# Layer norm beside two projection blocks: where statistics, transposes and weight splits stand in the order of work

## The chip, the cores and the metric

The kernel runs on one core of a Trainium2 chip. The metric is the device time of one execution in microseconds (us); lower is better. Three runs of the kernel before gave 1754.59, 1755.76 and 1760.3 us; the median is 1755.76 us. A fourth execution was recorded by the hardware profiler; it took 1754.43 us, and its span, from the first to the last instruction, is 1752.7 us.

## The reference

One sequence of 2048 rows of 512 values goes through attention with 32 heads of 16 and then through a two-layer network with SiLU, each behind a layer norm and each added to its input:

```python
x = A_x
h = x + _A_ref(_layernorm(x, axis=-1), A_wqkv, A_wo)
h2 = h + _B_ref(_layernorm(h, axis=-1), B_w1, B_w2)
```

`_A_ref` multiplies by `wqkv` (512 x 1536), splits into q, k and v, applies softmax over the scores, multiplies by v and by `wo`. The change concerns only the first layer norm and the product with `wqkv`.

## The kernel before

**Numbers.** Products are done on pairs of tiles in the engine's rounded 32-bit form: each operand is split into a high part, made by a copy on ScalarE (`act("copy", ...)`), and a low part, made by a subtraction on VectorE (`low`). A product takes three matmuls for each of four chunks: high by high, low by high, high by low (`product`, line 101). So one 128x512 result costs 12 matmuls.

**The stage around the change** (lines 281 to 422). The 2048 rows are treated in four blocks `b` of 512 rows, and each block in four tiles `t` of 128 rows. The rows of a block lie in `xts[b]`; only two such buffers exist, so blocks 0 and 2 share one (it is the memory of `ks[2]`), and blocks 1 and 3 the other. A tile has to pass four steps before the projections of its block can use it:

- `statistics` (line 147): two instructions on VectorE (`st`, then `mv`), then two small ones on GpSimd (`rs`, an addition and a power).
- `normalize` (line 158): one instruction on VectorE, which needs `rs`, and writes the rows in place.
- the transposes of `turn_x` (lines 161 and 363): four on TensorE into the PSUM tile `ps_tr`,
- a copy on ScalarE into `xth[b]` and a subtraction on VectorE into `xtl[b]`.

While block `b` is projected, the rows of block `b + 1` are put through these four steps. A block has six units `n`: two projections of group 0, 128 key columns and 128 query columns (`("qk", 1)` for k and `("qk", 0)` for q, 12 matmuls each with the whole 512 rows of `xth[b]` and `xtl[b]` as the streamed operand), and four for v (`("v", t)`, 12 matmuls each, with one tile's columns of `xth[b]` and `xtl[b]` as weights). Block 0 does the four v units first, the others the two qk units first. After a qk unit, ScalarE writes `sh` and VectorE writes `sl` from the PSUM tile, and both are stored to device memory; after unit `k == 0` the heads' rows are read back with `load_q` and `load_k`. From block 1 on, each v unit is followed by `burst(4)`: four score products (`ps_m`, four PSUM banks of five) and four row maxima on VectorE (`mx`, line 206). The results of the projections and of the transposes take turns in three PSUM banks.

**Weight splits.** `split_qk(n)` (line 314) splits columns of `wqkv` for group `n // 2`, query (`n` even) or key (`n` odd): one copy on ScalarE (`wqk_h`) and one subtraction on VectorE (`wqk_l`). Splits 1 and 0 are done ahead of the loop. The six others were taken from a list behind units 3, 4 and 5 of blocks 0 and 1. They are needed in the next stage (line 424), which projects groups 1 to 3. The unsplit weights lie in the tail of `va`, the tile that holds v: the query columns under the places of row chunks 8 to 12, the key columns under those of 12 to 15, so a v unit of block 2 or 3 may write only when the splits under it are done. One `memset` on GpSimd (line 422) fills a column of ones in `va` behind the loop.

**What sets the order.** Every instruction of TensorE, VectorE, ScalarE, GpSimd and the DMA queue on SyncE is kept in program order within its engine (`pin`, `dve`, `act`, `pool`, `mm`, `tr`, `dma`), so the order of the calls in the loop is the order on each engine. Engines wait for each other by semaphores.

**The next stage** (line 424) projects the remaining groups, with four score products and maxima behind every seven matmuls (`BESIDE_A = 7, 4`).

Of the kernel before, what the change touches and what calls it, by code (L numbers as in the profile page):

```python
# [28 lines left out]
NG = 2 * D // P  # L29
# [30 lines left out]
def attention_mlp_kernel(ctx: ExitStack, tc: tile.TileContext, x, wqkv, wo, w1, w2, out):  # L60
# [12 lines left out]
    def pool(op, *a, **k):  # L73
        tc.keep_in_program_order(getattr(nc.gpsimd, op)(*a, **k))  # L74
# [5 lines left out]
    def act(fn, *a, **k):  # L80
        pin(getattr(nc.scalar, fn)(*a, **k))  # L81

    def dve(fn, *a, **k):
        pin(getattr(nc.vector, fn)(*a, **k))  # L84
# [4 lines left out]
    def low(dst, src, high, engine="dve"):  # L89

        if engine == "pool":
            pool("tensor_tensor", dst, src, high.bitcast(F32), ALU.subtract)
        else:
            dve("tensor_tensor", dst, src, high.bitcast(F32), ALU.subtract)
# [52 lines left out]
    def statistics(rows):  # L147

        st = small.tile([P, 6], F32, name="st", bufs=5)
        mv = small.tile([P, 2], F32, name="mv", bufs=5)  # L150
        rs = small.tile([P, 1], F32, name="rs", bufs=5)
        dve("bn_stats", st, rows)
        dve("bn_aggr", mv, st)
        pool("tensor_scalar", rs, mv[:, 1:2], EPS, None, op0=ALU.add)
        pool("tensor_tensor", rs, rs, expo, ALU.pow)
        return mv, rs

    def normalize(dst, rows, mv, rs):
        dve("tensor_scalar", dst, rows, mv[:, 0:1], rs, op0=ALU.subtract, op1=ALU.mult)

    def turn(src, dst_h, dst_l):

        ps = bank("ps_tr").rearrange("p (c n) -> p c n", n=P)
        for c in range(4):
            tr(ps[:, c, :], src[:, c * P:(c + 1) * P], ident)
        act("copy", dst_h, ps)
        low(dst_l, ps, dst_h)
# [10 lines left out]
    def load_k(i, k, lo=0, n=S):  # L178
        a, j = HEADS[k]
        h = 4 * (i % 8) + 2 * a + j  # L180
        dma(ks[i % RING][64 * j:64 * j + 48, a, lo:lo + n], kd[:, h * DH:(h + 1) * DH, lo:lo + n])

    def load_q(i, k):
        a, j = HEADS[k]
        h = 4 * (i % 8) + 2 * a + j
        lo = i // 8 * 512
        dma(qs[i % RING][64 * j:64 * j + 48, a, :], qd[:, h * DH:(h + 1) * DH, lo:lo + 512])
# [58 lines left out]
    def tick():  # L246
        at["step"] += 1
        for fn, a in agenda.pop(at["step"], ()):
            fn(*a)
# [19 lines left out]
    def burst(n):  # L269
        for _ in range(n):  # L270
            one_max()
# [9 lines left out]
    with ExitStack() as pa:  # L281
# [18 lines left out]
        def load_x(b, parts=1):  # L300
            n = 4 // parts
            for t in range(0, 4, n):
                r0 = b * 512 + t * P
                dma(xts[b][:, t:t + n, :], x[r0:r0 + n * P, :].rearrange("(t p) d -> p t d", p=P))
# [9 lines left out]
        def split_qk(n):  # L314
            g, key = divmod(n, 2)
            raw = raw_qk[key][:, :, g * P:(g + 1) * P]
            cols = slice(key * D + g * P, key * D + (g + 1) * P)
            act("copy", wqk_h[:, :, cols], raw)
            low(wqk_l[:, :, cols], raw, wqk_h[:, :, cols])

        def measure():

            ps = bank("ps_sq")
            mm(ps[:, :NG], ones, sq, start=True, stop=True)
            dve("tensor_reduce", qk_s, ps[:, :NG], axis=AX.X, op=ALU.add)
            pool("tensor_scalar", qk_s, qk_s, 1e-30, None, op0=ALU.add)
            pool("tensor_tensor", qk_s, qk_s, expo, ALU.pow)
            dve("tensor_scalar", qk_s, qk_s, TOP / 23.0, None, op0=ALU.mult)
            dve("tensor_scalar", qk_s.bitcast(U32), qk_s.bitcast(U32), 0x7F800000, None, op0=ALU.bitwise_and)
            dve("reciprocal", qk_e, qk_s)  # L330
            dve("scalar_tensor_tensor", qk_e, qk_e, SCALE, qk_e, op0=ALU.mult, op1=ALU.mult)
            pin(nc.scalar.reg_load(qk_f, qk_e[:1, :].bitcast(U32)))

        def project_qk(b, n, beside=None):

            g, key = divmod(n, 2)
            cols = slice(key * D + g * P, key * D + (g + 1) * P)
            ps = bank("ps_qk")
            weave(product(ps, lambda c: wqk_h[:, c, cols], lambda c: wqk_l[:, c, cols],
                          lambda c: xth[b][:, c, :], lambda c: xtl[b][:, c, :], DC), beside)  # L340
            sh = xp.tile([P, 512], F16, name="sh")
            sl = xp.tile([P, 512], F16, name="sl", bufs=2)
            if beside:

                t = scaled[b]
                act("mul", t, ps, qk_s)
                act("copy", sh, t)
                pool("tensor_tensor", sl, t, sh, ALU.subtract)
            else:
                act("mul", sh, ps, qk_s)  # L350
                dve("scalar_tensor_tensor", sl, ps, qk_s, sh, op0=ALU.mult, op1=ALU.subtract)
            d = (kd if key else qd)[:, g * P:(g + 1) * P, b * 512:b * 512 + 512]
            hs, ls = (slice(0, 3, 2), 1) if key else (slice(0, 2), 2)
            dma(d[hs].rearrange("s d n -> d s n"), sh[:, None, :].to_broadcast([P, 2, 512]))
            dma(d[ls], sl)

        def project_v(b, t):
            ps = bank("ps_v")
            run(product(ps, lambda c: xth[b][:, c, t * P:(t + 1) * P], lambda c: xtl[b][:, c, t * P:(t + 1) * P],
                        lambda c: wv_h[:, c, :], lambda c: wv_l[:, c, :], DC))  # L360
            act("copy", va[:, 4 * b + t, :, 0:DH], ps.rearrange("p (h d) -> p h d", d=DH))

        def turn_x(b, t):
            turn(xts[b][:, t, :], xth[b][:, :, t * P:(t + 1) * P], xtl[b][:, :, t * P:(t + 1) * P])
# [10 lines left out]
        found = [statistics(xts[0][:, t, :]) for t in range(4)]  # L375
# [9 lines left out]
        for n in range(NG):  # L385
            square(n)

        splits = list(range(2, NG))
        for b in range(NB):
            units = [("qk", 1), ("qk", 0)]  # L390
            vs = [("v", t) for t in range(4)]
            found = {}
            for n, (kind, k) in enumerate(vs + units if b == 0 else units + vs):
                tick()
                if b == 0 and n == 3:
                    measure()
                if kind == "v":
                    project_v(b, k)
                else:
                    project_qk(b, k)  # L400
                    if k == 0:
                        for i in range(2):
                            for h in range(4):
                                if b == 0:
                                    load_q(i, h)
                                load_k(i, h, b * 512, 512)
                if b > 0 and n > 1:
                    burst(4)
                if b + 1 < NB:
                    rows = xts[b + 1]  # L410
                    if n < 4:
                        found[n] = statistics(rows[:, n, :])
                    if 0 < n < 5:
                        normalize(rows[:, n - 1, :], rows[:, n - 1, :], *found.pop(n - 1))
                    if n > 1:
                        turn_x(b + 1, n - 2)
                if n > 2 and b < 2 and splits:
                    split_qk(splits.pop(0))
                if n == 0 and b + 2 < NB:
                    load_x(b + 2)  # L420
        assert not splits
# [2 lines left out]
        for g in range(1, NG // 2):  # L424
            for m, (b, key) in enumerate([(b, 1) for b in range(NB)] + [(b, 0) for b in range(NB)]):
# [4 lines left out]
                n = 8 * g + m - 12  # L430
# [183 lines left out]
    found = {}  # L614
# [57 lines left out]
    def maxima(g):  # L672

        i, c = divmod(g, KC)
        if g < LAG:
            return 0
        ready = min(ITEMS, i + RING - (0 if c == KC - 1 else 1)) * 64
        rate = max([(64 * (n + 1) - BESIDE * sum(g <= m <= KC * n for m in marks) - at["done"])
                    / max(1, KC * n - AHEAD - g) for n in range(i + 1, ITEMS)] or [0])
        if ready < END:  # L680
            rate = min(rate, (ready - at["done"]) / (KC - 1 - c or KC))
        at["due"] += max(0, rate)
        n = max(0, min(4, int(at["due"]), ready - at["done"]))
        at["due"] -= n
        return n

    fixed_rows(RING - 1)
    for g in range(groups):
# [10 lines left out]
        if i in (8, 16, 24):  # L699
            b, n = i // 8 - 1, c - OUTPUT  # L700
# [13 lines left out]
        n = maxima(g)  # L714
# [43 lines left out]
```

## Time and profile before

| | before |
|---|---|
| median of three runs | 1755.76 us |
| profiled execution | 1754.43 us |
| its span | 1752.7 us |
| TensorE busy | 1699.7 us (97%) |
| VectorE busy | 1472.0 us (84%) |
| ScalarE busy | 1263.3 us (72%) |
| GpSimd busy | 208.4 us (12%) |
| mean granted TensorE clock | 0.992 |

In the profile PE is TensorE, PEld its weight loads, DVE VectorE, ACT ScalarE, POOL GpSimd and SP SyncE. A row of the timeline gives the start in us from the beginning of the span, the duration, the engine, the line, the operation, output and inputs, the count, and in square brackets how long the engine had been idle and what ended the wait. Matmuls are pipelined: their durations overlap, and the distance of two starts is what one costs in a stream. PEclk is the clock that TensorE was granted, as a share of full speed.

### The profile page before, as it was taken

The page shows a single profiled execution, that of the slowest core. Times are in us where ns is not written, and L with a number is a line of the kernel's source. Part 1 is how long each engine was busy: PE and PEld are TensorE (multiplying, and loading weights), DVE is VectorE, ACT ScalarE, POOL GpSimd, SP SyncE. Part 2 cuts the span into 40 slices and gives each one's busy share as a digit, 9 for nine tenths or more (in the row PEclk, how much of TensorE's full clock was granted, in tenths as well). Part 3 has the DMA queues.
Part 4 walks back from the last instruction along what each step waited for, and adds up shares of the span by engine and source line. Part 5 has one row for each costly group of instructions (what it writes and reads, how often), then busy time and mean ns, then how long its engine had stood idle before and what let it go on. Part 6 is the DMA issues. An engine that isn't in the chain of part 4 may idle for free.

```text
span 1752.7 us, 28228 instructions
## 1 busy us (share of the span) xinstructions
PE 1699.7 (97%) x10466; PEld 654.2 (37%) x10466; DVE 1472.0 (84%) x2456; ACT 1263.3 (72%) x2507; POOL 208.4 (12%) x216
## 2 busy tenths in 40 slices
PE   7899999999999999999999999999999999999899
PEld 6655422222245532222245532222245532221377
DVE  6889899999978889999978899999978889994243
ACT  4223499999963369999963269999963279999643
POOL 2112210000033300000033300000033200000000
PEclk9999999999999999999999999999999999999999
DMA  6233311111113111111213111111222111100232
GB/s 183 91 87 137 113 36 44 38 39 48 51 52 100 57 45 32 35 41 44 58 48 100 55 48 30 35 45 40 61 69 82 49 45 34 36 8 11 64 90 74
DMA packets 102210, 103.10 MB, mean 59 GB/s; under 512 B 20344, under 2 KB 78776, under 8 KB 102072
## 3 DMA queue, kind: packets, MB, share of 16 engines
q1 hardware_dynamic: 102072, 101.30, 19.8%
q8 instruction: 82, 1.34, 0.3%
q14 instruction: 56, 0.46, 0.1%
HBM read 77.86 MB, written 17.30 MB: 54 GB/s over the span
## 4 chain that ended last, share of the span: by engine, by line
PE 46%; ACT 33%; DVE 18%; DMA 1%; issue 1%; SPq 1%; POOL 0%; ACTq 0%; POOLq 0%; DVEq 0%
ACT pt L81 31%; PE pv L67 20%; DVE mx L206 13%; PE ps_s L67 9%; PE ps_m L67 6%; PE ps_acc L67 5%; PE ps_wo L67 2%; DVE gl L84 2%; PE ps_v L67 2%; PE ps_qk L67 1%; ACT pvs L81 1%; DVE ot L84 1%; SPq L87 1%; PE ps_tr L70 1%; DMA w<-in_B_w_dram 0%
## 5 line engine op out<-in xcount | busy, mean ns | idle before, releaser
L206 DVE TENSOR_REDUCE mx<-ps_m 128x1 f32<-128x512 f32 x2048 | 1280.4, 683 | 114.2 <-PE ps_m L67 87.8
L81 ACT ACTIVATE pt<-ps_s 128x512 f32<-128x512 f32 x2048 | 1017.7, 646 | 31.9 <-PE ps_m L67 31.4
L67 PE MATMUL ps_s<-qs,ks 64*128 64x512 f16 x2048 | 549.9, 380 | 10.6 <-ACT pt L81 2.4
L67 PE MATMUL ps_m<-ks,qs 48*128 48x512 f16 x2048 | 531.1, 381 | 11.6 <-DVE mx L206 8.9
L67 PE MATMUL pv<-pt,va 128*17 128x512 f32 x4096 | 539.0, 599 | 0.9
L67 PEld LDWEIGHTS <-ks 64*128 64x128 f16 x2048 | 152.4, 94 | 549.9 <-issue 443.5
L67 PEld LDWEIGHTS pv<-pt,va 128*17 128x17 f32 x4096 | 68.8, 95 | 240.3 <-issue 225.9
L67 PEld LDWEIGHTS <-qs 48*128 48x128 f16 x2048 | 122.1, 94 | 82.8 <-issue 77.1
L81 ACT ACTIVATE g<-pv 128x512 f32<-128x512 f32 x52 | 31.1, 597 | 146.3 <-PE pv L67 146.3
L74 POOL TENSOR_TENSOR ot<-ot,den 128x512 f32<-128x512 f32 x15 | 19.1, 1275 | 938.3 <-DMA den<-dr 938.3
L84 DVE TENSOR_TENSOR gl<-g,gh 128x512 fp32r<-128x512 f32 x56 | 59.0, 1053 | 44.1 <-ACT gh L81 44.1
L67 PE MATMUL ps_acc<-w2h,gh 128*128 128x512 f32 x224 | 92.3, 412 | 0.0
L67 PE MATMUL ps_acc<-w2l,gh 128*128 128x512 f32 x224 | 91.6, 409 | 0.0
L81 ACT CAST w2h<-w 128x512 fp32r<-128x512 f32 x56 | 34.8, 621 | 75.2 <-POOL w1l L74 38.7
L67 PE MATMUL ps_acc<-w2h,gl 128*128 128x512 f32 x224 | 88.1, 393 | 0.0
L67 PE MATMUL pv<-hth,w1l 128*128 128x512 f32 x208 | 86.6, 416 | 0.0
L67 PE MATMUL pv<-htl,w1h 128*128 128x512 f32 x208 | 82.8, 398 | 0.0
L67 PE MATMUL pv<-hth,w1h 128*128 128x512 f32 x208 | 82.8, 398 | 0.0
L74 POOL TENSOR_TENSOR w1l<-w,w1h 128x512 fp32r<-128x512 f32 x42 | 54.7, 1301 | 165.1 <-ACT w1h L81 154.8
L81 ACT ACTIVATE ks<-ps_qk,qk_s 128x512 f32<-128x512 f32 x24 | 16.5, 689 | 70.4 <-PE ps_qk L67 70.4
L74 POOL TENSOR_TENSOR w2l<-w,w2h 128x512 fp32r<-128x512 f32 x42 | 53.6, 1277 | 59.2 <-ACT w2h L81 59.2
L67 PE MATMUL ps_qk<-xtl,wqk_h 128*128 128x512 f32 x128 | 52.8, 413 | 3.4 <-DVE xtl L84 3.4
(99 smaller groups left out, 1162.6 us busy)
## 6 DMA issues: line engine op xcount, KB each, us to landing
w<-in_B_w_dram SPq DMA_DIRECT2D x112, 256.0 KB
ks<-kd SPq DMA_DIRECT2D x120, 192.0 KB
qs<-qd SPq DMA_DIRECT2D x128, 48.0 KB
kd<-sh SPq DMA_DIRECT2D x16, 256.0 KB
qd<-sh SPq DMA_DIRECT2D x16, 256.0 KB
ot<-pvs SPq DMA_DIRECT2D x128, 32.0 KB
den<-dr SPq DMA_DIRECT2D x128, 32.0 KB
hx<-in_A_x_dram SPq DMA_DIRECT2D x16, 256.0 KB
```

The source lines that it names most:

```text
L67: tc.keep_in_program_order(nc.tensor.matmul(*a, **k))
L70: tc.keep_in_program_order(nc.tensor.transpose(*a))
L74: tc.keep_in_program_order(getattr(nc.gpsimd, op)(*a, **k))
L81: pin(getattr(nc.scalar, fn)(*a, **k))
L84: pin(getattr(nc.vector, fn)(*a, **k))
L87: pin(nc.sync.dma_start(*a))
L206: pin(nc.vector.tensor_reduce(mx[i][:, j, a, qt, kb:kb + 1], ps, axis=AX.X, op=ALU.max))
```

## The change

```diff
-        splits = list(range(2, NG))
+        splits = {(0, 3): 2, (0, 4): 4, (0, 5): 6, (1, 5): 3, (3, 0): 5, (3, 1): 7}
+
+        first_ln = {n: (range(4)[n:n + 1], range(4)[max(0, n - 1):n], range(4)[max(0, n - 2):max(0, n - 1)])
+                    for n in range(6)}
+        other_ln = {0: ((0, 1), (0,), ()), 1: ((2, 3), (1,), (0,)), 2: ((), (2,), (1,)), 3: ((), (3,), (2,)),
+                    4: ((), (), (3,)), 5: ((), (), ())}
         for b in range(NB):
...
                 if b + 1 < NB:
                     rows = xts[b + 1]
-                    if n < 4:
-                        found[n] = statistics(rows[:, n, :])
-                    if 0 < n < 5:
-                        normalize(rows[:, n - 1, :], rows[:, n - 1, :], *found.pop(n - 1))
-                    if n > 1:
-                        turn_x(b + 1, n - 2)
-                if n > 2 and b < 2 and splits:
-                    split_qk(splits.pop(0))
+                    stats, norms, turns = (other_ln if b else first_ln)[n]
+                    for t in stats:
+                        found[t] = statistics(rows[:, t, :])
+                    for t in norms:
+                        normalize(rows[:, t, :], rows[:, t, :], *found.pop(t))
+                    for t in turns:
+                        turn_x(b + 1, t)
+                if (b, n) in splits:
+                    split_qk(splits.pop((b, n)))
                 if n == 0 and b + 2 < NB:
                     load_x(b + 2)
```

Block 0 keeps its layer-norm order (`first_ln` gives for every unit what the old conditions gave). In blocks 1 and 2 the statistics of tiles 0 and 1 stand in unit 0 with the normalisation of tile 0, those of tiles 2 and 3 in unit 1 with the normalisation of tile 1; the transposes of tiles 0 to 3 stand in units 1 to 4 instead of 2 to 5. Block 0 still makes three splits in units 3 to 5, now 2, 4, 6 (the query columns) instead of 2, 3, 4. Block 1 makes one (3, in unit 5) instead of three (5, 6, 7 in units 3 to 5). The last two, 5 and 7, stand in units 0 and 1 of block 3. On TensorE the four transposes of a tile therefore stand ahead of a v unit's 12 matmuls and its four score products, where they stood behind them. No instruction is added or removed.

## The prediction

> **What bounds the kernel now.** I read the page first, then the busy time in stretches of 20 us (the stretch, its length, then the busy time of PE, PEld, DVE, ACT and POOL with their instructions, the granted clock, the busy share of the DMA engines, GB/s).
>
> ```profile
> span 1752.7 us, 28228 instructions
> PE 1699.7 (97%) x10466; PEld 654.2 (37%) x10466; DVE 1472.0 (84%) x2456; ACT 1263.3 (72%) x2507; POOL 208.4 (12%) x216
> ```
>
> ```profile
> 40.00:60.00 20.00, 17.51 (x87) 11.78 (x85) 18.24 (x35) 6.94 (x12) 3.76 (x8) 1.00 0.45 138
> 60.00:80.00 20.00, 19.33 (x86) 14.20 (x87) 13.98 (x27) 4.90 (x8) 4.49 (x9) 0.91 0.22 71
> 80.00:100.00 20.00, 18.24 (x83) 12.84 (x82) 12.05 (x20) 3.73 (x6) 0.25 (x1) 1.00 0.16 54
> 120.00:140.00 20.00, 20.00 (x93) 11.50 (x92) 20.00 (x35) 5.72 (x9) 5.28 (x5) 1.00 0.33 109
> ```
>
> The 97% says nothing of the place that changes. That is about 35 to 105 us, blocks 1 to 3. There TensorE has holes, and from 60 to 80 its clock is at 0.91; afterwards VectorE is full. The chain of waits (start, us, what) shows which of them sets the time:
>
> ```profile
> 60.58 6.91 PE ps_qk L67 x22
> ...
> 85.64 5.30 PE ps_qk L67 x22
> ...
> 104.48 12.05 DVE mx L206 x20
> ```
>
> Through blocks 2 and 3 the chain is TensorE's projections; from 104.48 it is VectorE's row maxima without a break. What block 3 finishes sooner, that run starts sooner, and everything behind it moves with it.
>
> **What the change removes: the two block ends.** At both, TensorE waits for the copy and the subtraction of the last tile (`xth`, `xtl`). Its timeline at the ends of blocks 1 and 2, and at the end of block 3, which has no transposes:
>
> ```profile
> 55.69 0.61 PE L67 MATMUL ps_m<-ks,qs 48*128 48x512 f16 x4
> 56.39 0.66 PE L70 MATMUL ps_tr<-ident,ks 128*128 128x128 f32 x4
> 57.73 0.51 PE L67 MATMUL ps_qk<-xth,wqk_h 128*128 128x512 f32 x1 [0.68 <-ACT xth L81]
> ...
> 60.58 0.50 PE L67 MATMUL ps_qk<-xtl,wqk_h 128*128 128x512 f32 x1 [2.13 <-DVE xtl L84]
> ...
> 67.33 0.39 PE L67 MATMUL ps_v<-wv_h,xth 128*128 128x512 f32 x1
> ...
> 81.95 0.61 PE L67 MATMUL ps_m<-ks,qs 48*128 48x512 f16 x4
> ...
> 83.82 0.50 PE L67 MATMUL ps_qk<-xth,wqk_h 128*128 128x512 f32 x1 [0.68 <-ACT xth L81]
> ...
> 85.64 0.50 PE L67 MATMUL ps_qk<-xtl,wqk_h 128*128 128x512 f32 x1 [1.08 <-DVE xtl L84]
> ...
> 90.77 0.39 PE L67 MATMUL ps_v<-wv_h,xth 128*128 128x512 f32 x1
> ...
> 104.04 0.61 PE L67 MATMUL ps_m<-ks,qs 48*128 48x512 f16 x4
> ...
> 104.92 0.40 PE L67 MATMUL ps_qk<-xth,wqk_l 128*128 128x512 f32 x1
> ```
>
> Without a wait, the third matmul of a block starts 104.92 - 104.04 = 0.88 us after the last score products, plus one matmul's distance of 0.23 (the 22 matmuls from 85.64 to 90.77 take 5.13): 1.11. Block 1 took 60.58 - 55.69 = 4.89, block 2 took 85.64 - 81.95 = 3.69. Of each, 0.41 is the transposes, which only move (74.98 - 74.57 below). Lost: 4.89 - 1.11 - 0.41 = 3.37 and 3.69 - 1.11 - 0.41 = 2.17. With the transposes of tile 3 in unit 4, `xtl` of tile 3 is a whole v unit ahead of the block end, and both go.
>
> **The clock behind the first of them.** The 22 matmuls from 60.58 to 67.33 take 6.75 instead of 5.13, which is 1.62 us more, because the clock was halved (stretches of 2 us, same columns):
>
> ```profile
> 62.00:64.00 2.00, 2.00 (x6) 1.55 (x5) 0.00 (x0) 0.00 (x0) 0.00 (x0) 0.50 0.14 49
> 64.00:66.00 2.00, 2.00 (x9) 1.64 (x8) 0.60 (x1) 0.69 (x1) 0.00 (x0) 0.82 0.00 1
> ```
>
> I take these 1.62 as removed with the hole of 2.13 us ahead of them. The Trainium skill (TensorE: Matmul & The Clock Gate, HAM oscillation) gives as its abstract rule that holes under some 3.4 us don't throttle; this trace disagrees, since 2.13 us after 0.68 did. The same page (Part 1) has the activity window running freely, so that the halving would vary between runs; by that the 1.62 might be missing elsewhere, and the sum would be 1.62 smaller. Both are priced as a rival below from rows alone.
>
> **Small waits inside the units.** A unit without a wait:
>
> ```profile
> 74.03 0.61 PE L67 MATMUL ps_m<-ks,qs 48*128 48x512 f16 x4
> 74.57 0.66 PE L70 MATMUL ps_tr<-ident,ks 128*128 128x128 f32 x4
> 74.98 0.48 PE L67 MATMUL ps_v<-wv_h,xth 128*128 128x512 f32 x1
> 75.29 0.39 PE L67 MATMUL ps_v<-wv_h,xtl 128*128 128x512 f32 x1
> ...
> 78.61 0.66 PE L70 MATMUL ps_tr<-ident,ks 128*128 128x128 f32 x4
> ```
>
> Score products to transposes is 0.54; at 55.69 it is 0.70, because the normalisation is late. The transposes of tile 2 in both blocks cost about as much more. With a wait of the first score products of block 1 of like size, I take four times 0.16 = 0.63 as removed. The next unit starts 3.88 us after this one (78.61 less 0.16, less 74.57). VectorE per unit needs less than that:
>
> ```profile
> 73.79 0.52 DVE L84 TENSOR_SCALAR ks<-ks,mv,rs 128x512 f32<-128x512 f32 x1
> 74.22 0.68 DVE L84 TENSOR_TENSOR xtl<-ps_tr,xth 128x512 fp32r<-128x512 f32 x1
> 74.82 2.47 DVE L206 TENSOR_REDUCE mx<-ps_m 128x1 f32<-128x512 f32 x4
> 77.22 0.68 DVE L84 BATCH_NORM_STATS2 st<-ks 128x6 f32<-128x512 f32 x1
> ```
>
> From the normalisation to the end of the maxima it is 77.22 - 73.79 = 3.43 us, 0.45 below TensorE's 3.88, so units 2 to 5 of the changed blocks are paced by TensorE. In the old block 1 the statistics (0.84) and a split (0.60) came on top, which is why VectorE ended behind.
>
> **What the change adds: one new wait in each of blocks 1 and 2.** The transposes of tile 0 now stand in unit 1, directly behind the second qk projection, and they need tile 0's normalisation. VectorE, GpSimd and TensorE there:
>
> ```profile
> 18.78 0.69 DVE L84 BATCH_NORM_STATS2 st<-ks 128x6 f32<-128x512 f32 x1 [2.43 <-DMA ks<-in_A_x_dram]
> 20.69 0.55 DVE L84 TENSOR_SCALAR ks<-ks,mv,rs 128x512 f32<-128x512 f32 x1 [0.20 <-POOL rs L74]
> ...
> 39.79 0.68 DVE L84 BATCH_NORM_STATS2 st<-ks 128x6 f32<-128x512 f32 x1
> 40.92 0.39 PE L67 MATMUL ps_v<-wv_h,xth 128*128 128x512 f32 x1
> 41.09 0.57 POOL L74 TENSOR_TENSOR rs<-rs,expo 128x1 f32<-128x1 f32 x1
> ```
>
> Block 0 already runs the new sequence (statistics of two tiles, then a normalisation that waits for `rs`): from 18.78 to 20.69 + 0.55 = 21.24 it took 2.46 us. Started at 39.79 (it can't start sooner, `sl` of the first projection stands ahead of it), it ends at 42.25. TensorE is there at 40.92. It waits 1.33 us, and behind the transposes stand the whole first v unit and its score products, so nothing covers it. The power on GpSimd, over at 41.66, bounds it from below: 41.66 + 0.55 - 40.92 = 1.29. From above, were another 0.5 us lost on GpSimd, 1.8. Block 2 has the same order and the same 1.33. The v unit behind the transposes has a first matmul of 0.31 instead of 0.23 (75.29 - 74.98), 0.1 for each block. Added: 2 x 1.43 = 2.86.
>
> Does the new wait halve the clock? Holes of 0.68 and 1.08 us close to each other, at 83.82 and 85.64, left it at 1.00; the 2.13 at 60.58 did not. 1.33 in one piece is nearest to the first, so I take nothing; the other end is 1.62 for each block.
>
> **What the moves cost elsewhere.** On VectorE, `sl` of the second projection now follows the normalisation and starts at about 42.2, some tenths later, and its store on the DMA queue follows; in block 1 that queue still issues the reads of heads until 49 (the row of 48.35 below), so nothing waits. The first maxima come behind the statistics of four tiles, but the score products also come 1.33 + 0.41 later. On ScalarE `xth` of tile 0 goes ahead of the copy of the first v, no conflict. PSUM has three banks: the second v unit now takes the bank of the transposes just ahead, whose `xtl` I put about 0.9 us before it is needed; if late, it costs at most the lateness.
>
> In block 2 the statistics of the last block's rows are read sooner, at about 62.2 instead of 66.07. Their load is issued behind those reads:
>
> ```profile
> 48.35 0.67 SPq L87 DMA_DIRECT2D ks<-kd  x1
> ...
> 50.10 0.41 SPq L87 DMA_DIRECT2D ks<-in_A_x_dram  x1
> ```
>
> By the stretches above, DMA traffic has ebbed to 49 GB/s by 62 to 64 and is 1 GB/s from 64; the remaining trickle is the reading of heads, which is used only at the first score products. I take nothing.
>
> The splits: three in block 0 stay three, nothing. Two leave block 1, and go behind the two projections of block 3:
>
> ```profile
> 91.69 0.75 DVE L84 SCALAR_TENSOR_TENSOR sl<-ps_qk,qk_s,sh 128x512 f16<-128x512 f32 x1 [1.97 <-ACT sh L81]
> 94.01 2.49 DVE L206 TENSOR_REDUCE mx<-ps_m 128x1 f32<-128x512 f32 x4 [1.57 <-PE ps_m L67]
> ```
>
> VectorE is idle for 1.97 and 1.57 us there, and a split takes 0.60 to 0.68; ScalarE is busy 3.73 of the 20 us from 80. The copy of block 3's first v must wait for the last split, which ends at 91.69 + 0.75 + 0.68 = 93.1 on the old axis, before the first maxima. The fill of ones on GpSimd waits for the same split; GpSimd is busy 0.25 of those 20 us. Nothing for all of them; without the cover it would be 0.68 for each split.
>
> **The sum.** Removed 3.37 + 2.17 + 1.62 + 0.63 = 7.79; added 2.86; net 4.93 us. Against the profiled execution, span 1752.7 plus 1.73 around it, that is 1754.43 - 4.93 = 1749.5. The median of the runs shown is 1.33 above that execution; carried over whole, 1750.8. I forecast 1750.0, between them. The bound for a change that can be told from none, 0.3%, is 1755.76 x 0.997 = 1750.5, so the forecast lies just beyond it.
>
> **Rivals.**
>
> - *The clock takes part of it back.* The new waits halve the clock in one block (1749.5 + 1.62 = 1751.1) or both (1752.7); or the removed halving is peculiar to this execution, worth the same 1.62. For it: 1.33 lies between 1.08 and 2.13. Against: the longer sum of two holes at 82 to 86 left the clock alone, and no run shown is below the profiled one, which had the halving. About 1751.9.
> - *The start of VectorE's long run doesn't move.* If something else, such as reading the heads of block 3, sets the start at 104.48, the net gain is lost: 1754.4 to 1755.8. Against: the chain shows a v unit and its score products ahead of that run, and no DMA.
> - *Slower: the rows of the last block come late.* The place is the first statistics of block 2, now at 62.2. VectorE would stand there, with `sl` and the normalisation behind it, and TensorE before the transposes. It could be at most 66.07 - 62.2 = 3.9 us, since before the statistics ran at 66.07 without a wait. In each further hole of such length the clock is halved, 1.62 for one stretch and 3.2 for two. 3.9 + 3.2 = 7.1 against 4.93 gives 1756.6; with one halving it decides from 4.93 - 1.62 = 3.3 us of lateness on. If the new wait of block 1 also reaches its upper end (0.5 more, and 1.62), 1758.7; measured against the median that is 0.2% slower, and more if the median carries its 1.33. Against: the traffic ebbs by 64.
>
> **How the numbers follow.** The forecast has 0.72, and by its own range of 1748.0 to 1751.5 (one halving more removed in block 2, or small waits kept) 0.56 of that lies beyond 0.3% and 0.16 within. The clock rival has 0.12 and the unmoved run 0.07, both within. The slower rival, with what I don't see, has 0.09: 0.06 slower by over 0.3%, 0.03 within. Together faster 0.56, same 0.38, slower 0.06. The range, 1747.0 to 1755.0, takes in the clock's bounds and half of the unmoved run.
>
> **What would show it.** In blocks 1 and 2 one hole of about 1.3 us ahead of the transposes, released by the normalisation on VectorE, and no hole over 0.3 us at the block ends; the clock at 1.00 through 60 to 70; units of 3.9 us; the unbroken run of maxima starting near 99.6 instead of 104.48, and later landmarks as much sooner. Wrong would be: holes over 2 us at the new place, v units longer than 4 us, a wait of block 2's statistics for the DMA, or a run of maxima that starts sooner while the end doesn't move.

## The result and the profile after

The changed kernel takes 1749.97 us in the median of 13 runs (1745.81 to 1753.83); the kernel before takes 1755.76 us in the median of 13 runs (1754.59 to 1760.3). The ratio is 0.9964, 95% interval 0.9956 to 0.9972, which is 4.9 to 7.7 us. The profiled execution took 1749.97 us, 4.46 us less than the profiled one before.

The page of the changed kernel, first part:

```profile
span 1748.2 us, 28230 instructions
PE 1695.7 (97%) x10466; PEld 651.4 (37%) x10466; DVE 1471.9 (84%) x2456; ACT 1263.6 (72%) x2507; POOL 207.4 (12%) x216
```

The engines' work is the same (all five counts are equal; the two instructions more in the first line are on none of these engines). The stretches of 20 us (columns as in the prediction) show where the time left:

```profile
40.00:60.00 20.00, 18.75 (x94) 13.09 (x93) 17.62 (x34) 5.90 (x10) 3.41 (x8) 1.00 0.46 137
60.00:80.00 20.00, 18.75 (x95) 13.16 (x93) 16.84 (x32) 5.83 (x10) 3.42 (x8) 1.00 0.21 72
80.00:100.00 20.00, 20.00 (x92) 13.96 (x90) 13.24 (x22) 4.98 (x9) 1.01 (x1) 1.00 0.32 76
```

TensorE does 94 and 95 instructions in the first two stretches, where it did 87 and 86; the clock from 60 to 80 is 1.00 instead of 0.91. The chain of waits through blocks 1 and 2 (start, us, what):

```profile
35.54 5.34 PE ps_qk L67 x22
40.88 1.23 issue
42.11 0.63 PE ps_tr L70 x4
...
57.14 0.54 PE ps_m L67 x4
57.68 5.68 PE ps_qk L67 x24
...
80.16 5.67 PE ps_qk L67 x24
...
99.37 12.05 DVE mx L206 x20
```

Apart from the new waits the chain now stays on TensorE from block 1 to block 3, with no step of `xtl` at their ends. The new wait begins at 40.88. TensorE's timeline and VectorE's at that place:

```profile
40.48 0.39 PE L67 MATMUL ps_qk<-xtl,wqk_h 128*128 128x512 f32 x1
42.11 0.63 PE L70 MATMUL ps_tr<-ident,ks 128*128 128x128 f32 x4 [1.25 <-issue]
42.49 0.47 PE L67 MATMUL ps_v<-wv_h,xth 128*128 128x512 f32 x1
42.81 0.39 PE L67 MATMUL ps_v<-wv_h,xtl 128*128 128x512 f32 x1
...
57.08 0.61 PE L67 MATMUL ps_m<-ks,qs 48*128 48x512 f16 x4
57.61 0.50 PE L67 MATMUL ps_qk<-xth,wqk_h 128*128 128x512 f32 x1
57.95 0.39 PE L67 MATMUL ps_qk<-xth,wqk_l 128*128 128x512 f32 x1
58.18 0.40 PE L67 MATMUL ps_qk<-xtl,wqk_h 128*128 128x512 f32 x1
...
64.60 0.63 PE L70 MATMUL ps_tr<-ident,ks 128*128 128x128 f32 x4 [1.25 <-ACT sh L81]
```

```profile
39.56 0.68 DVE L84 BATCH_NORM_STATS2 st<-ks 128x6 f32<-128x512 f32 x1
...
41.46 0.55 DVE L84 TENSOR_SCALAR ks<-ks,mv,rs 128x512 f32<-128x512 f32 x1 [0.20 <-POOL rs L74]
```

The third matmul of block 2 follows the last score products by 58.18 - 57.08 = 1.10 us (4.89 before). The two new waits are 1.25 us each. The trace names `issue` and `sh` as what ended them, but the transposes read neither; what they need is the normalisation, which ends at 41.46 + 0.55 = 42.01, just ahead of 42.11. That this is the wait's cause is tested below, by moving the normalisation and the transposes.

The executions differ already ahead of the changed place: the granted clock first rises at 16.92 us before and at 16.18 after. So the stage is measured from the product of the sums of squares (`ps_sq`, in block 0) to the start of VectorE's long run of maxima. Before, that is 104.47 - 23.81 = 80.66 us; after, 99.36 - 23.53 = 75.83. The stage is 4.83 us shorter.

### The profile page after: what moved, and what is told of

Read it like the earlier page. It is cut to its first block, busy times and chain, and to the rows that moved or that the text cites. A ratio compares the mean times of both kernels' runs of the same rounds, so it can differ in the third digit from the quotient of the medians.

```text
span 1748.2 us, 28230 instructions
## 1 busy us (share of the span) xinstructions
PE 1695.7 (97%) x10466; PEld 651.4 (37%) x10466; DVE 1471.9 (84%) x2456; ACT 1263.6 (72%) x2507; POOL 207.4 (12%) x216
## 4 chain that ended last, share of the span: by engine, by line
PE 48%; ACT 32%; DVE 16%; issue 1%; DMA 1%; SPq 1%; ACTq 0%; POOLq 0%; POOL 0%; DVEq 0%
ACT pt L81 30%; PE pv L67 20%; DVE mx L206 12%; PE ps_s L67 9%; PE ps_m L67 6%; PE ps_acc L67 5%; PE ps_v L67 3%; PE ps_wo L67 2%; DVE gl L84 2%; PE ps_qk L67 2%; PE ps_tr L70 1%; DVE ot L84 1%; ACT pvs L81 1%; SPq L87 1%; PE ps_w L67 0%
## 5 line engine op out<-in xcount | busy, mean ns | idle before, releaser
L74 POOL TENSOR_TENSOR w2l<-w,w2h 128x512 fp32r<-128x512 f32 x42 | 53.5, 1275 | 59.5 <-ACT w2h L81 59.5
L67 PE MATMUL ps_qk<-xth,wqk_h 128*128 128x512 f32 x128 | 52.5, 411 | 0.8 <-ACT xth L81 0.8
```

Of the source, the lines that this page charges most:

```text
L67: tc.keep_in_program_order(nc.tensor.matmul(*a, **k))
```

## The experiments

"Stage" is the distance just defined, read from one profiled execution of each kernel. Each ratio is to runs of the kernel before that were made beside that kernel (medians from 1755.55 to 1756.44 us); 5 to 13 runs stand behind each median.

| kernel | stage, us | median, us | ratio to before, 95% interval |
|---|---|---|---|
| before | 80.66 | 1755.76 | |
| the change | 75.83 | 1749.97 | 0.9964 (0.9956 to 0.9972) |
| e1_order_only | 75.80 | 1750.13 | 0.9970 (0.9959 to 0.9982) |
| e2_splits_only | 77.69 | 1753.25 | 0.9984 (0.9973 to 0.9995) |
| e3_first_turn_later | 73.44 | 1749.02 | 0.9963 (0.9949 to 0.9976) |
| e4_four_statistics | 79.86 | 1753.97 | 0.9988 (0.9979 to 0.9997) |
| e5_block2_only | 79.59 | 1752.52 | 0.9984 (0.9972 to 0.9996) |
| e6_later_again | 73.41 | 1748.04 | 0.9962 (0.9949 to 0.9974) |
| e7_all_ends | 74.16 | 1749.67 | 0.9964 (0.9949 to 0.9980) |
| e8_keys_first | 72.72 | 1746.72 | 0.9946 (0.9932 to 0.9959) |

**The order of layer norm alone** (e1_order_only).

```diff
-        splits = {(0, 3): 2, (0, 4): 4, (0, 5): 6, (1, 5): 3, (3, 0): 5, (3, 1): 7}
+        splits = {(0, 3): 2, (0, 4): 3, (0, 5): 4, (1, 3): 5, (1, 4): 6, (1, 5): 7}
```

> New order of layer norm in blocks 1 and 2, but the six weight splits where they stood before (2, 3, 4 behind units 3 to 5 of block 0; 5, 6, 7 behind units 3 to 5 of block 1). My theory: with `xtl` of the last tile a unit ahead of the block end, two more splits of 0.60 us on VectorE in block 1 still end before they are missed, so this is as fast as the change as a whole: start of VectorE's long run of maxima near 99.4 us, 4.5 to 5 us below before. Rival (the gain comes from taking two splits out of block 1): a wait of TensorE for `xtl` over 0.3 us at the end of block 1 stays, and at least 1.2 us of the gain is lost.

The stage is 75.80 us, the same as with the whole change, and the only waits of TensorE over 0.3 us in blocks 1 to 3 are these two:

```profile
42.85 0.63 PE L70 MATMUL ps_tr<-ident,ks 128*128 128x128 f32 x4 [1.25 <-issue]
...
65.34 0.63 PE L70 MATMUL ps_tr<-ident,ks 128*128 128x128 f32 x4 [1.26 <-ACT sh L81]
```

There is no wait at the ends of blocks 1 and 2. The rival falls: with the new order the splits may stand in block 1.

**The splits alone** (e2_splits_only).

```diff
-                    stats, norms, turns = (other_ln if b else first_ln)[n]
+                    stats, norms, turns = first_ln[n]
```

> Old order of layer norm in all blocks, with the splits where the change puts them. My theory: VectorE reaches the last `xtl` of block 1 two splits (1.2 us) sooner; the hole of 2.13 us shrinks to about 1.0 to 1.3, the clock stays at 1.00 behind it (1.62 us), the end of block 2 keeps its waits of 0.68 and 1.08, and no new wait comes: start of the long run near 101.6, 2.8 us below before (1.2 if the clock is halved all the same). Rival (the splits' move does nothing): 104.2 and the time of before.

The stage is 77.69 us, 2.97 less than before. The end of block 1 and the clock behind it:

```profile
57.40 0.50 PE L67 MATMUL ps_qk<-xth,wqk_h 128*128 128x512 f32 x1 [0.68 <-ACT xth L81]
...
59.21 0.50 PE L67 MATMUL ps_qk<-xtl,wqk_h 128*128 128x512 f32 x1 [1.08 <-DVE xtl L84]
```

```profile
60.00:62.00 2.00, 2.00 (x10) 1.61 (x9) 0.00 (x0) 0.15 (x1) 0.00 (x0) 1.00 0.20 72
```

The hole is 1.08 instead of 2.13 us, and the clock stays at 1.00. So in these profiles the splits' move by itself is worth about 3 us, some 1.6 of it by the clock, and the new order by itself 4.86, yet both together only 4.83: they remove the same wait at the end of block 1, and whichever comes second finds it gone.

**Block 2 alone** (e5_block2_only).

```diff
-                    stats, norms, turns = (other_ln if b else first_ln)[n]
+                    stats, norms, turns = (other_ln if b == 2 else first_ln)[n]
```

with the splits as in the first experiment.

> New order of layer norm in block 2 only; block 1 and the six splits as before. My theory prices this part at 2.17 + 0.16 removed at the end of block 2 and 1.43 added by the new wait, net 0.9 us: the waits of 0.68 and 2.13 at the end of block 1 stay, those at the end of block 2 go, one wait of 1.25 comes in block 2; from TensorE's first wait at the end of block 0 to the start of the long run of maxima 68.7 us (before: 69.57, the change: 64.73), if the clock is halved behind block 1 as in the profile before, and 67.1 if not. Median 0.9 us below before, less than these rounds can tell. Rival (the end of block 2 carries half of the gain of the change): 67.1 with the clock halved, 2.4 below before.

From the first wait at the end of block 0 (33.91) to the long run (102.33) it is 68.42 us, 1.15 less than before; 68.7 was expected. (From `ps_sq`, as in the table, it is 1.07 less.) The end of block 1 is as before, and the clock was halved behind it for 3.4 us from 59.5; in block 2 there is the new wait only:

```profile
59.45 0.76 PE L67 MATMUL ps_qk<-xtl,wqk_h 128*128 128x512 f32 x1 [2.13 <-DVE xtl L84]
...
67.57 0.63 PE L70 MATMUL ps_tr<-ident,ks 128*128 128x128 f32 x4 [1.24 <-issue]
```

The price of the part fits in the stage. By the ratio the whole run is 2.8 us shorter, but the interval reaches from 0.7 to 4.9 and holds the part's 1.1 as well as the rival's 2.4. At this size the time of whole runs doesn't settle it, the stage does.

**The new wait made longer** (e4_four_statistics).

```diff
-        other_ln = {0: ((0, 1), (0,), ()), 1: ((2, 3), (1,), (0,)), 2: ((), (2,), (1,)), 3: ((), (3,), (2,)),
+        other_ln = {0: ((0, 1, 2, 3), (0,), ()), 1: ((), (1,), (0,)), 2: ((), (2,), (1,)), 3: ((), (3,), (2,)),
```

> The change, with the statistics of all four tiles in unit 0, ahead of the first normalisation: the suspected new wait made longer. My theory: the normalisation of tile 0 ends 1.2 to 1.3 us later in blocks 1 and 2, and TensorE's hole grows from 1.25 to about 2.5 us in each. Time 2.5 us above the changed kernel if the clock stays, and 1.6 us more for each block in which it is halved behind the hole (5.7 in all), start of the long run between 101.9 and 105. Rival (the wait is covered by slack later): within 1 us of the changed kernel.

The stage is 79.86 us, 4.03 above the change. The two holes are alike, and what follows them is not (waits, then stretches of 2 us):

```profile
42.54 1.08 PE L70 MATMUL ps_tr<-ident,ks 128*128 128x128 f32 x4 [2.53 <-issue]
...
67.84 0.63 PE L70 MATMUL ps_tr<-ident,ks 128*128 128x128 f32 x4 [2.52 <-issue]
```

```profile
44.00:46.00 2.00, 2.00 (x7) 1.57 (x6) 0.69 (x1) 0.25 (x1) 0.00 (x0) 0.54 0.20 64
...
68.00:70.00 2.00, 2.00 (x12) 1.72 (x12) 1.55 (x3) 0.59 (x1) 0.47 (x1) 1.00 0.19 66
```

2 x 1.28 us of longer holes are 2.56. The remaining 1.47 is near what one halving cost before (1.62), and there is one, behind the first hole only. Nothing covers the wait: the median too is 4.00 us above that of the change, so the rival, slack, falls.

**The new wait taken away** (e3_first_turn_later and e6_later_again, the same kernel).

```diff
-        other_ln = {0: ((0, 1), (0,), ()), 1: ((2, 3), (1,), (0,)), 2: ((), (2,), (1,)), 3: ((), (3,), (2,)),
+        other_ln = {0: ((0, 1), (0,), ()), 1: ((2, 3), (1,), ()), 2: ((), (2,), (0, 1)), 3: ((), (3,), (2,)),
```

> The change, but the transposes of tile 0 stand in unit 2 ahead of those of tile 1, so none follows the second qk projection directly. My theory: the two new waits of 1.25 us go, with the restart behind them, and nothing takes their place: start of the long run near 96.6, 2.5 to 2.8 us below the changed kernel, 7.5 below before. Rival (the wait only moves to the next v unit, because VectorE has two tiles' `xtl` to write in unit 2): waits of 0.5 us or more ahead of the second v unit, and under 1.5 us of gain over the changed kernel.

> The kernel of the run with the first transposes in unit 2 once more. Its profile had the long run of maxima 2.4 us nearer to TensorE's first wait than the changed kernel, as expected, but lost 3.85 us between 192 and 212 us to halved clock, and its median was only 0.95 below the changed kernel's. Theory (chance: the clock's windows lie anew in every execution): the distance is 62.3 again, the halvings lie at other places or fewer, and over both sets of runs the kernel is 2 to 2.7 us below the changed one. Rival (the new order itself brings the halvings at 193 and 207, in most executions): both come again, and the gain over the changed kernel stays under 1 us.

The stage is 73.44 us in the first execution and 73.41 in the second, 2.4 less than the change, near the two waits' 2.5. No wait of TensorE over 0.3 us is left from behind the end of block 0 to the long run. In the first execution that gain was given back between 193 and 213 us, where the clock was halved for four stretches of 3.4 us; the changed kernel's profile has one there, and so has the second execution. Only one of the two halvings came again, so the rival is not borne out. The medians are 1749.02 and 1748.04. Over both sets (13 runs) the median is 1748.21, 1.76 below that of the change: less than the 2 to 2.7 expected, more than the rival's 1. The ratios to before tell the two kernels apart even less (0.9963 and 0.9962 against 0.9964). With runs that spread over 8 us, the gain in the stage is shown, and that the whole run is shorter for it is not.

**All block ends** (e7_all_ends). Block 0's own end had waits of 0.82 and 0.17 us in every kernel so far. With the edit before:

```diff
+        first_ln = {0: ((0,), (), ()), 1: ((1,), (0,), ()), 2: ((2,), (1, 2), (0,)), 3: ((3,), (3,), (1, 2)),
+                    4: ((), (), (3,)), 5: ((), (), ())}
```

> The same kernel, and in block 0 the transposes of tiles 0, 1 and 2, 3 stand in units 2, 3, 3, 4 and the normalisations of tiles 2 and 3 in units 2 and 3, so that the end of block 0 has no transposes either. My theory: the last known waits, 0.82 and 0.17 at the end of block 0, go; start of the long run 3.3 to 3.7 us earlier in its block stage than the changed kernel, median 3 to 4 us below it, near 1746.3. Rival (VectorE, waiting for GpSimd's power ahead of two normalisations in block 0, holds up the first projections): waits of 0.5 us or more ahead of units 3 to 5 of block 0, and no gain over the run with the first transposes in unit 2.

Neither theory held: the stage is 74.16 us, 0.7 longer than without this edit. The waits at the end of block 0 went, but now TensorE waits for a transfer, the heads of block 0 read back (`ks<-kd`), at the first score products:

```profile
44.08 0.61 PE L67 MATMUL ps_m<-ks,qs 48*128 48x512 f16 x4 [2.01 <-DMA ks<-kd]
```

The last store ahead of the reads, and the last of the four reads that the products need, without the edit (e3_first_turn_later, `ps_sq` at 24.76) and with it (`ps_sq` at 23.11):

```profile
36.15 0.33 SPq L87 DMA_DIRECT2D qd<-sl  x1
...
40.75 0.67 SPq L87 DMA_DIRECT2D ks<-kd  x1
```

```profile
35.45 0.33 SPq L87 DMA_DIRECT2D qd<-sl  x1
...
40.63 0.67 SPq L87 DMA_DIRECT2D ks<-kd  x1
```

Counted from `ps_sq`, the read is issued at 17.52 us, 1.5 later than without the edit (15.99). The store is 0.95 us later: two tiles' transposes instead of one stand between `ps_sq` and the first qk projection, with a wait of 0.27 behind them. The other 0.6 passes between the store and the reads; what it is made of was not traced. And TensorE arrives 1.0 us sooner (18.96 instead of 19.95, the wait taken off), because the waits that covered the transfer went. The next run (e8_keys_first) moves the reads of the keys ahead of the reads that wait for the queries:

```diff
-                            for h in range(4):
-                                if b == 0:
-                                    load_q(i, h)
-                                load_k(i, h, b * 512, 512)
+                            for h in range(0, 4, 2):
+                                for m in range(2):
+                                    load_k(i, h + m, b * 512, 512)
+                                for m in range(2):
+                                    if b == 0:
+                                        load_q(i, h + m)
```

> The kernel without transposes at any block end, whose first score products waited 2.01 us for the heads read back in block 0 (the last of the four reads they need was issued at 40.63 and its data were there at 44.08). Here the reads of the key rows of two heads are issued ahead of those of their query rows, in pairs, so that they go out while the store of the queries is still under way. Theory (that wait is the queue's: a store, four reads of 0.7 us in a row, then the landing): the last of the four reads is issued 1.4 us sooner, the wait shrinks from 2.01 to 0.5 to 1.0 us, and from the product of the sums of squares (ps_sq) to the start of the long run of maxima it takes 72.6 to 73.2 us (74.16 without this, 73.4 with the block end of block 0 as before, 75.8 in the change). Rival (the landing is what lasts, whatever the order of issue): the wait stays at 1.8 us or more. In the time of whole runs 1 us is not to be told.

TensorE's row, and the DMA queue's issues ahead of it:

```profile
43.06 0.61 PE L67 MATMUL ps_m<-ks,qs 48*128 48x512 f16 x4 [0.55 <-DMA qs<-qd]
```

```profile
36.33 1.63 SPq L87 DMA_DIRECT2D ks<-kd  x2
38.78 1.40 SPq L87 DMA_DIRECT2D qs<-qd  x2
```

The keys' reads go out while the queries' store is under way; the wait is 0.55 instead of 2.01 us, and the stage is 72.72, as expected. That most of the wait was the queue's order, and not the landing, is shown. The stage is the shortest of all, and so is the median, 1746.72 us, from five runs; but the interval of its ratio (0.9932 to 0.9959) overlaps those of e6 and e7, so the time of whole runs doesn't show that it is faster than those two.

## Why the prediction was right

- *The block ends* (3.37 and 2.17). Gone: 1.10 us from the last score products to the third matmul, where 1.11 was put as the time without a wait. With block 1 left as it was, block 2's part alone (the end, a small wait and the new wait) was put at 0.9 and measured 1.15.
- *The clock behind the first* (1.62). Gone in every profile without the hole: it came back with the 2.13 us hole when block 1 was left as it was, and stayed away when the splits' move cut the hole to 1.08. But the prediction took the whole 1.62 as certain, and only two profiles have this hole. The last section shows a longer hole that did not halve the clock, so that every execution of the kernel before lost these 1.62 is not shown.
- *Small waits in the units* (0.63). Gone; in the trace after, score products to transposes is 0.53 or 0.54 in every unit. One of the four was counted twice, though: the 0.16 from 55.69 to 56.39 already lies in the 4.89 from which 3.37 was taken. Without it the sum is 4.77.
- *The new waits* (1.33 each, with 0.1 for the restart). The trace's 1.25 is idle time alone. Counted from start to start, as 1.33 was, the transposes stand at 42.11 where the v unit would have been at 40.48 + 0.23 = 40.71, which is 1.40, and the first v matmul takes 0.32 instead of 0.23. So the price was right to a tenth. The time taken from block 0's same sequence, 2.46 us from the first statistics to the end of the normalisation, was 42.01 - 39.56 = 2.45 in block 1.
- *The clock behind the new waits* (nothing). The clock stayed at 1.00 through 40 to 100. Made twice as long, the wait was followed by a halved clock in one of two cases, for about 1.5 us; so the mechanism of the first rival exists, and its price of 1.62 was near.
- *The splits* (nothing). Right for the change as a whole. What the prediction did not say is that the move alone would have brought 3 us: it is redundant here.
- *The slower rival.* The statistics of block 2 began at 62.06, right behind `sl`, without a wait for the rows; nothing of it came.
- *The sum.* 4.93 was predicted for the stage (4.77 without the double count), 4.83 was measured. The profiled executions differ by 4.46: the stage began 0.28 sooner after the change, and 0.65 was lost behind the stage.
- *The time.* The forecast of 1750.0 against a median of 1749.97 is luck to that nearness. The sum gave 1749.5 from the profiled execution and 1750.8 from the median of three runs, 1750.0 was chosen between them, and the 13 executions of the changed kernel spread over 8 us. The medians are 5.79 us apart, 0.96 more than the stage; what the rest comes from was not shown.

One sign of the prediction did not hold: that later landmarks would be as much sooner. The shift is whole up to 190 us, and then moves in steps. The rows that end an item, which is 64 row maxima on VectorE (`nm`), before and after, at the third, the twelfth and the thirteenth item:

```profile
194.47 0.22 DVE L213 TENSOR_REDUCE nm<-mx 128x16 f32<-128x64 f32 x1
...
636.13 0.22 DVE L213 TENSOR_REDUCE nm<-mx 128x16 f32<-128x64 f32 x1
...
680.56 0.22 DVE L213 TENSOR_REDUCE nm<-mx 128x16 f32<-128x64 f32 x1
```

```profile
189.36 0.22 DVE L213 TENSOR_REDUCE nm<-mx 128x16 f32<-128x64 f32 x1
...
631.22 0.22 DVE L213 TENSOR_REDUCE nm<-mx 128x16 f32<-128x64 f32 x1
...
674.06 0.22 DVE L213 TENSOR_REDUCE nm<-mx 128x16 f32<-128x64 f32 x1
```

5.11, 4.91 and then 6.50 us sooner: in the kernel before the clock was halved once between the last two, and after it was not. The stretches of 15 us from 630, before and then after, have the clock at 0.89 and 1.00:

```profile
630.00:645.00 15.00, 14.28 (x77) 4.80 (x76) 12.76 (x24) 10.36 (x22) 0.00 (x0) 0.89 0.20 72
```

```profile
630.00:645.00 15.00, 14.31 (x105) 3.61 (x107) 14.26 (x26) 14.59 (x31) 0.00 (x0) 1.00 0.09 25
```

At 1015 to 1030 it is the other way round, and 1.4 us go back. Smaller steps of 0.1 to 0.4 us between other items were not traced. The large steps are of the same size as what a part of the change is worth.

## What to carry to other kernels

Price a reordering by the first instruction that must wait in the new place, and take that price from another place of the same trace where the same sequence already runs: 2.46 us from block 0 gave the new wait to a tenth. Two edits that shorten the same wait don't add up, so test each alone; and a wait that goes may have covered another one, as the end of block 0 covered part of the reading back of the heads. Where single runs spread more than the edit is worth, compare a stage between two landmarks of the profile.

## What was not expected of the hardware

Every halving of TensorE's clock in these profiles is 3.413 us long or a multiple of it (the one that the end of a profile cuts off aside), and within one execution their starts lie on one grid of that step, counted from the first rise of the clock, which is at another time in each execution (11.7 to 18.9 us). The record of the clock for the run with four statistics in unit 0 (start in us, length in us, share of full speed):

```
15.111  27.307  1.0
42.418   3.413  0.5
```

From 15.111 to 42.418 it is 27.307 us, eight steps of 3.413. The hole of 2.53 us that ends at 42.54 lies, all but its last 0.1 us, in one step of that grid, and the clock was halved at the step's end. The equal hole that ends at 67.84 is cut by the grid at 66.3 into about 1.0 and 1.5 us, and the clock was not halved behind it. In blocks 1 to 3 of all ten profiles, the steps that were followed by a halving held 2.1 to 2.6 us of TensorE's waits, the others at most 1.5. The hole of 2.13 us before the change lies whole in the step from 57.88 to 61.30, and the clock was halved at 61.30. The Trainium skill (TensorE: Matmul & The Clock Gate, Part 1) describes such a free-running window of 3413 ns, and this trace agrees with it; the section on HAM oscillation puts the danger at holes over some 3.4 us, and here 2.13 and 2.53 us were enough when they fell into one step.

Waits alone are not the whole rule. Ahead of the halving at 638.15 us in the kernel before, the step holds one wait of 0.68 us, at 637.43, among products that use 48 or 64 of the 128 rows:

```profile
637.43 0.37 PE L67 MATMUL ps_m<-ks,qs 48*128 48x512 f16 x1 [0.68 <-DVE mx L206]
```

Why the clock was halved there was not shown.

One and the same kernel takes different times. Of the changed kernel's 13 executions, the five with a mean clock of 0.995 took 1745.81 to 1749.09 us, and the four with 0.991 took 1750.63 to 1753.83. That the halvings make all of this spread was not shown.
